# Writing the first batch of a fused attention and MoE kernel as one fixed order on five queues

## The chip, the core and the metric

The kernel runs on one core of a Trainium2 chip. The core has a matrix engine (TensorE, in the profile PE, with its weight loads as PEld) and three engines for other arithmetic: VectorE (DVE), ScalarE (ACT) and GpSimd (POOL). A fifth queue, SP, issues the transfers (DMA) between the chip's main memory and the core's memory. Each queue works strictly in its own order: an instruction that waits holds up everything behind it on the same queue. Only waits on other queues' results join them. The metric is the time of one execution in microseconds (us) on the device, taken from several runs.

## The reference

The inputs are `q`, `k`, `v` (8 batches, 8 heads, 576 rows, 64 columns), `p` (8, 8, 32, 64), and two weight matrices `w_in` (512 x 2048) and `w_out` (2048 x 512), which come as 64-bit floats.

```python
def sm_attn(qq, kk, vv):
    s = scale * np.matmul(qq, kk.transpose(0, 1, 3, 2))
    s = s - np.max(s, axis=-1, keepdims=True)
    a = np.exp(s)
    a = a / (np.sum(a, axis=-1, keepdims=True) + 1e-09)
    return np.matmul(a, vv)
p_packed = sm_attn(p, k, v)
out = sm_attn(q, p_packed, p_packed)
...
h = x @ w_in
relu6 = np.clip(h + 3.0, 0.0, 6.0)
g = h * relu6 / 6.0
return (g @ w_out)
```

`x` is the attention's result, its heads side by side: 4608 rows (8 batches of 576) of 512 columns.

## The kernel before

The 2048 columns between the two weight matrices are cut into 16 slices of 128; slice f is called **tile f** here. For each batch the kernel first does the attention. It never forms the attention's final product: the second softmax `a` (kept as `a_hi`, `a_lo`) is multiplied with `m`, the product of the packed values `pp` with `w_in`. Numbers are split into a rounded part and a rest (`hi`, `lo`), so each product is three matmuls.

**The first batch** is special, because the weights arrive while it runs. `first_attention` computes the attention of batch 0. `first_moe` then goes through the 16 tiles. Names for the steps of tile f, with their lines in the kernel before:

- **gemm1(f)** (L451, PE): 12 matmuls of 288 columns into the accumulator `ps_h`, of which there is one (`bufs=1`).
- **m0(f)** (`u_m0`, L196 PE, L207 ACT, L209 DVE): `m` for tile f. Its matmuls take one of two small accumulators (`ps_a0`, two buffers), which the attention of batch 1 uses as well.
- **relu(f)** (L954, ACT) and **stt(f)** (L955, DVE): the gate, read from `ps_h`. gemm1(f+1) can't start before stt(f) has let `ps_h` go.
- **gh(f)** (L963, ACT), the small `bnd_hi` (L964), and **gl(f)** (L965, POOL): the split of the gate.
- **gemm2(f)** (L856, PE): 12 matmuls of 512 columns. It stands one tile later in the order.
- **Narrowing in f** and **out f** (`narrowed`, L128): the 64-bit words of a slice of `w_in` or `w_out` become 32-bit: two passes on ACT (L142, L144), a shift on DVE (L148, after the first of the two passes), an add on POOL (L152). For `w_out` follow **wo_hi** (L162, ACT) and **wo_lo** (L164, on DVE, or on POOL for tiles 8 to 12).

The raw words land in two buffers each for `w_in` and `w_out` (`wp`, `bufs=2`); tiles 2 and 3 have places of their own. So the load of a slice waits on SP until the POOL add of the slice two before it is done.

**Attention of batch 1** runs between these tiles: transposes `tr` of the blocks of k and q on DVE (L401), scores **s1** (L268 PE, copies L284 ACT, maxima L285 DVE, exponentials L293 ACT), their transposes **et** (L307 PE, L308 ACT), the packed values **pv** (L323 PE), and the second scores **s2** (`u_s2`, L354): L268 on PE, then on DVE a transpose (L359); then, for each of two halves of the heads (`u_a`), a maximum and a subtraction (L367, L368, DVE), an exponential (L369, ACT), sum, add, reciprocal, product and transpose (L372 to L378, DVE), a_hi (L381, ACT) and a_lo (L383, DVE).

**What sets the order.** `first_attention` and the first four tiles stand in an order written out by hand on PE, DVE, ACT and POOL (`tc.manual_schedule(engines=HAND)`). From tile 4 on (`IN_ORDER = 4`) a scheduler, which has a model of its own of the times, orders these queues, and SP everywhere. `attend` hands it one and then two steps of the attention of batch 1 per tile. Batches 1 to 7 (`moe`, L864) are ordered by the scheduler before and after; there the attention of the next batch runs between tiles, as `fill` hands it out.

Of the kernel before, what the change touches and what calls it, by code (L numbers as in the profile page):

```python
# [36 lines left out]
def packed_attention_moe(  # L37
# [120 lines left out]
    def w_out_step(f):  # L158
# [5 lines left out]
        (nc.gpsimd if f in POOL else nc.vector).tensor_sub(out=wo_lo[:, f], in0=x, in1=wo_hi[:, f].bitcast(F32))  # L164
# [227 lines left out]

    def attention(b):


        def load(which, a):
            state["nat", which, b, a] = load_blocks(k if which == "k" else q, b, a)

        def turn(which, a):
            t = ap.tile([P, T, 32], F32, name="tr", tag="tr", bufs=4)  # L400
            nc.vector.transpose(out=t, in_=state.pop(("nat", which, b, a)))  # L401
            state[which, b, a] = t
# [56 lines left out]
    def first_attention():  # L459
# [336 lines left out]
        rest(m1)
        rest(b1)
        rest(wout0)
        step(wout1, 2)
        gemm1(h, 0, 1)  # L800
        warm(WARM[4])
        return h, {2: win2}, {1: wout1, 2: wout2}

    HAND = {mybir.EngineType.PE, mybir.EngineType.DVE, mybir.EngineType.Activation, mybir.EngineType.Pool}
# [92 lines left out]
    def first_moe(h, w_in, w_out):  # L897

        ahead = attention(1) if B > 1 else iter(())
        accs, m0 = [], {}  # L900
# [140 lines left out]
```

## Time and profile before

| what | value |
|---|---|
| median of 3 runs | 763.76 us (761.15 to 763.96) |
| the profiled execution | 758.97 us |
| its span, first to last instruction | 757.1 us |
| mean granted clock of TensorE | 0.995 of full |
| busy: PE, DVE, ACT, POOL | 739.4, 336.3, 387.6, 282.3 us |
| first product of batch 1 on PE starts | 138.26 us |

A row of the timeline has the start and the length in us, the queue, the line, the operation with its output and inputs, and in brackets how long the queue was idle before it and what ended the wait. Rows of equal instructions that follow each other are merged (x12). Float32 matmuls are counted twice each. A row of a window has its start and end, its length, the busy time of PE, PEld, DVE, ACT and POOL with counts, the granted clock of TensorE, the share of the DMA engines and GB/s. A row of a group has line, queue, operation, shapes and count, then busy us, mean ns of one, and the idle time before them. Lengths of instructions that follow each other overlap a little; the distance from start to start is what one costs.

### The profile page before, as it was taken

Reading aid. Unit: us, or ns where it says so; the run is one execution under the profiler, and the core shown is the slowest. Engines: PE = TensorE matmul, PEld = TensorE weight load, DVE = VectorE, ACT = ScalarE, POOL = GpSimd, SP = SyncE. Lnnn points to the kernel's source line nnn. Section 1 sums busy time; section 2 is a strip of 40 time slices with the busy share of each in tenths; the row PEclk is TensorE's granted clock in tenths of the full one; section 3 lists DMA queues with packets and bytes.
Section 4 is the critical chain, followed back from the end, with each engine's and each line's share of the span. In section 5 each row is a group of like instructions: output and inputs, shape, how many; then the busy total and the mean of one; then the engine's idle time right before and its main releaser. Section 6 shows DMA issues by size and latency. Waiting matters only on the chain.

```text
span 757.1 us, 13994 instructions
## 1 busy us (share of the span) xinstructions
PE 739.4 (98%) x5197; PEld 583.4 (77%) x5197; DVE 336.3 (44%) x709; ACT 387.6 (51%) x922; POOL 282.3 (37%) x420
## 2 busy tenths in 40 slices
PE   8998898999999999999999999999999999999998
PEld 6775675768777877888777886788787887888886
DVE  3676648432463355342733446342643527321121
ACT  4677864644455446463455535463354635553343
POOL 0487973423233233332333223333333333343332
PEclk9999899999999999999999999999999999999999
DMA  9859983104420532043310524024220210000010
GB/s 257 261 144 218 237 223 63 56 9 88 102 37 29 103 67 52 1 88 71 63 43 1 114 53 82 1 58 98 47 61 1 61 33 29 1 29 0 2 42 29
DMA packets 191205, 55.98 MB, mean 74 GB/s; under 512 B 173216, under 2 KB 184480, under 8 KB 191136
## 3 DMA queue, kind: packets, MB, share of 16 engines
q1 hardware_dynamic: 191136, 55.08, 31.6%
q8 instruction: 41, 0.67, 0.4%
q14 instruction: 28, 0.23, 0.1%
HBM read 45.61 MB, written 9.44 MB: 73 GB/s over the span
## 4 chain that ended last, share of the span: by engine, by line
PE 83%; DMA 5%; DVE 4%; SPq 3%; ACT 3%; issue 1%; POOL 1%; DVEq 0%; POOLq 0%; ACTq 0%
PE acc L856 47%; PE ps_hh L827 23%; PE ps L268 6%; SPq L216 2%; DMA raw_in<-in_moe_w_in_dram 2%; PE ps L323 2%; DMA nat<-in_k_dram 1%; PE ps_h L451 1%; DVE tr L401 1%; PE ps L307 1%; SPq L254 1%; POOL x_out L152 1%; PE ps_w L639 1%; DMA raw_out<-in_moe_w_out_dram 1%; DMA spare<-in_k_dram 1%
## 5 line engine op out<-in xcount | busy, mean ns | idle before, releaser
L845 POOL TENSOR_TENSOR g<-t,g 128x256 fp32r<-128x256 f32 x224 | 167.5, 751 | 410.7 <-ACT g L844 384.5
L856 PE MATMUL acc<-wo_hi,g 128*128 128x512 f32 x896 | 316.4, 394 | 1.3 <-ACT g L844 1.3
L840 DVE SCALAR_TENSOR_TENSOR t<-t,ps_hh 128x320 f32<-128x320 f32 (+1 forms) x224 | 100.1, 449 | 251.8 <-ACT t L839 251.6
L839 ACT ACTIVATE t<-ps_hh,three 128x320 f32<-128x320 f32 (+1 forms) x224 | 112.4, 503 | 177.9 <-PE ps_hh L827 169.8
L856 PEld LDWEIGHTS acc<-wo_hi,g 128*128 128x128 f32 x896 | 167.7, 188 | 35.4 <-issue 3.5
L856 PE MATMUL acc<-wo_lo,g 128*128 128x512 f32 x448 | 177.6, 396 | 0.0
L844 ACT CAST g<-t 128x256 fp32r<-128x256 f32 x224 | 90.4, 405 | 93.9 <-DVE t L840 92.6
L827 PE MATMUL ps_hh<-a_hi,m_hi 128*128 128x320 f32 (+1 forms) x448 | 136.2, 304 | 0.3 <-DVE t L840 0.3
L827 PE MATMUL ps_hh<-a_lo,m_hi 128*128 128x320 f32 (+1 forms) x448 | 132.7, 296 | 0.0
L827 PE MATMUL ps_hh<-a_hi,m_lo 128*128 128x320 f32 (+1 forms) x448 | 132.7, 296 | 0.0
L827 PEld LDWEIGHTS ps_hh<-a_hi,m_hi 128*128 128x128 f32 x448 | 84.4, 188 | 34.4 <-issue 19.9
L856 PEld LDWEIGHTS acc<-wo_lo,g 128*128 128x128 f32 x448 | 84.5, 189 | 12.4 <-issue 2.1
L827 PEld LDWEIGHTS ps_hh<-a_lo,m_hi 128*128 128x128 f32 x448 | 84.5, 189 | 8.2 <-issue 0.9
L827 PEld LDWEIGHTS ps_hh<-a_hi,m_lo 128*128 128x128 f32 x448 | 84.5, 189 | 1.6 <-issue 1.3
L401 DVE STREAM_TRANSPOSE tr<-nat 128x576 f32<-128x576 f32 x56 | 41.8, 765 | 30.2 <-DMA nat<-in_q_dram 12.8
L391 DVE TENSOR_TENSOR m_lo<-ps,m_hi 128x512 fp32r<-128x512 f32 x56 | 36.1, 684 | 35.1 <-ACT m_hi L390 35.1
L851 POOL TENSOR_TENSOR bnd_lo<-t,bnd_hi 128x64 fp32r<-128x64 f32 x112 | 39.1, 349 | 0.0
L390 ACT CAST m_hi<-ps 128x512 fp32r<-128x512 f32 x56 | 30.0, 589 | 9.9 <-PE ps_hh L827 8.1
L268 PE MATMUL ps<-w_in_sb,pps 64*32 64x512 f32 x448 | 34.3, 601 | 0.6 <-DVE m_lo L391 0.6
L856 PE MATMUL acc<-wo_hi,gh 128*128 128x512 f32 x64 | 26.7, 417 | 2.7 <-ACT gh L963 2.7
L152 POOL TENSOR_TENSOR w_in_sb<-w_in_sb,raw_in 128x512 int32<-128x512 int32 x14 | 18.9, 1347 | 27.7 <-ACT raw_in L144 19.2
L965 POOL TENSOR_TENSOR gl<-t,gh 128x512 fp32r<-128x512 f32 x16 | 22.0, 1373 | 17.6 <-ACT bnd_hi L964 11.0
...
## 6 DMA issues: line engine op xcount, KB each, us to landing
...
nat<-in_k_dram SPq DMA_DIRECT2D x112, 72.0 KB, 2.6
nat<-in_q_dram SPq DMA_DIRECT2D x112, 72.0 KB, 2.5
...
```

Source lines behind the costliest of these rows:

```text
L152: nc.gpsimd.tensor_tensor(out=xi, in0=xi, in1=low, op=ALU.add)
L268: nc.tensor.matmul(banks[x][NPK * a:NPK * a + NPK, :n], rows[half, a], c, start=True, stop=True)
L390: nc.scalar.copy(out=hi[:, x], in_=ps)
L391: nc.vector.tensor_sub(out=lo[:, x], in0=ps, in1=hi[:, x].bitcast(F32))
L401: nc.vector.transpose(out=t, in_=state.pop(("nat", which, b, a)))
L827: nc.tensor.matmul(h[:, :n], mm[:, g, fs], aa[:, t0:t0 + n], start=(g == 0 and i == 0), stop=(g == NG - 1 and i == 2),)
L839: nc.scalar.activation(out=t[:, :n], in_=h, func=AF.Relu, bias=three)
L840: nc.vector.scalar_tensor_tensor(out=t[:, :n], in0=t[:, :n], scalar=6.0, in1=h, op0=ALU.min, op1=ALU.mult)
L844: nc.scalar.copy(out=gh, in_=tm)
L845: nc.gpsimd.tensor_sub(out=gl, in0=tm, in1=gh.bitcast(F32))
L851: nc.gpsimd.tensor_sub(out=bnd_lo[:, slot:slot + REM], in0=tb, in1=bh.bitcast(F32))
L856: nc.tensor.matmul(acc, gg, ww[:, f], start=(f == 0 and i == 0), stop=(f == NF - 1 and i == 2),)
```

## The change

All of the first batch, `first_attention` and the 16 tiles, now stands in one written order, and on SP too. The diff, cut to what matters:

```diff
-WARM = (3, 2, 2, 1, 3)
+WARM = (3, 2, 2, 2)
...
-                raw = wp.tile([P, DM * (2 if wide_in else 1)], I32 if wide_in else F32, name=f"raw_{name}")
+                raw = wp.tile(
...
+                    bufs=3 if name == "in" else 2,
+                )
...
-        (nc.gpsimd if f in POOL else nc.vector).tensor_sub(out=wo_lo[:, f], in0=x, in1=wo_hi[:, f].bitcast(F32))
+        nc.vector.tensor_sub(out=wo_lo[:, f], in0=x, in1=wo_hi[:, f].bitcast(F32))
...
+    def first_parts(b):
...
+        return [
+            [[], [lambda: transpose_p(b), tn("k", 0), ld("k", 2), tn("k", 1), ld("k", 3)], []],
...
+            [[], [], [go(s2)]],
+            [[go(s2)], [], [go(s2)]],
+            [[go(s2)], [], [go(s2)]],
...
-        step(wout0, 3)
-        step(win1, 2)
...
+        load_w(4, ("in",))
+        if B > 1:
+            load_p(1)
+            load("k", 1, 0)
+            load("k", 1, 1)
...
-        win2, wout2 = w_in_step(2), w_out_step(2)
-        step(win2, 2)
-        step(wout2, 2)
...
-        def attend(f, n):
-            if f >= FIRST_AHEAD:
-                for _ in range(n):
-                    next(ahead, None)
+        def attend(f, place):
+            for part in plan[f][place] if f < len(plan) else ():
+                part()
...
-            if f == IN_ORDER:
-                hand.close()
...
-            step(in_(f + 2), 4)
...
-            rest(out_(f + 1))
-            step(out_(f + 2), 3 if f else 1)
...
+            attend(f, 1)
+            for i in (3, 4) if f == 3 else (f + (f > 3),):
+                rest(out_(i))
+            rest(in_(f + 2))
+            if f > 1:
+                more("in", f + 5)
+            for i in (3, 4) if f == 2 else (f + 1 + (f > 2),):
+                step(out_(i), 4)
+                if i not in (2, 3):
+                    more("out", 5 if i == 1 else i + 2)
             if last:
                 gemm2(*last)
...
+            with tc.issue_after(state["load"].ins):
+                for _ in range(PER_STEP if s < NF + FPC - 1 else 1000):
```

In tile f each queue now gets, in this order: the plan's first place; gemm1(f) and the matmuls of m0(f+1); relu, stt, the rest of m0(f+1), gh, bnd, gl; the plan's second place; wo_hi and wo_lo of tile f+1 (of tile f in tiles 0 to 2, of both 3 and 4 in tile 3); the narrowing of in f+2; the narrowing of out f+2 up to the POOL add (out f+1 in tiles 0 and 1, out 3 and out 4 in tile 2); gemm2(f-1); the plan's third place. The load of in f+5 is issued behind the narrowing of in f+2 (three buffers), that of out f+4 behind the narrowing of out f+2. The work of batch 2 is ordered behind the last weight load by `issue_after`; the scheduler still places it, on the five queues, between the written instructions. `warm` are matmuls on zeros.

The names in the rows below: `t` is the gate, `raw_140` and `raw_143` the raw words of tiles 2 and 3, `raw_in` and `raw_out` those of the others, `x_out` a narrowed slice of `w_out`, `z` and `at` the two forms of the second softmax. Lines of the changed kernel have other numbers: relu is L954 before and L987 after, stt L955 and L988, wo_hi L162 and L158, narrowing L142, L144, L148, L152 and L138, L140, L144, L148.

**ACT between relu(0) and relu(1).** Before:

```order
L954 ACTIVATE t<-ps_h_456,three 128x576
L162 CAST wo_hi<-x_out 128x512
L963 CAST gh<-t 128x512
L964 CAST bnd_hi<-t 128x64
L142 ACTIVATE raw_143<-raw_143 128x512
L144 ACTIVATE raw_143<-raw_143 128x512
L954 ACTIVATE t<-ps_h_534,three 128x576
```

After:

```order
L987 ACTIVATE t<-ps_h_456,three 128x576
L994 CAST gh<-t 128x512
L995 CAST bnd_hi<-t 128x64
L158 CAST wo_hi<-x_out 128x512
L138 ACTIVATE raw_140<-raw_140 128x512
L140 ACTIVATE raw_140<-raw_140 128x512
L138 ACTIVATE raw_out<-raw_out 128x512
L140 ACTIVATE raw_out<-raw_out 128x512
L987 ACTIVATE t<-ps_h_554,three 128x576
```

The narrowing of in 2 (`raw_140`) stood ahead of relu(0) before; it now stands behind gh(0) and wo_hi(0).

**ACT between relu(11) and relu(12).** Before:

```order
L954 ACTIVATE t<-ps_h_1314,three 128x576
L963 CAST gh<-t 128x512
L964 CAST bnd_hi<-t 128x64
L162 CAST wo_hi<-x_out 128x512
L142 ACTIVATE raw_in<-raw_in 128x512
L144 ACTIVATE raw_in<-raw_in 128x512
L142 ACTIVATE raw_out<-raw_out 128x512
L144 ACTIVATE raw_out<-raw_out 128x512
L207 CAST m_hi<-ps_1327 128x2x128
L162 CAST wo_hi<-x_out 128x512
L954 ACTIVATE t<-ps_h_1390,three 128x576
```

After:

```order
L987 ACTIVATE t<-ps_h_1324,three 128x576
L203 CAST m_hi<-ps_1337 128x2x128
L994 CAST gh<-t 128x512
L995 CAST bnd_hi<-t 128x64
L158 CAST wo_hi<-x_out 128x512
L138 ACTIVATE raw_in<-raw_in 128x512
L140 ACTIVATE raw_in<-raw_in 128x512
L138 ACTIVATE raw_out<-raw_out 128x512
L140 ACTIVATE raw_out<-raw_out 128x512
L377 CAST a_hi<-at 128x576
L987 ACTIVATE t<-ps_h_1388,three 128x576
```

A step of the second softmax of batch 1, a_hi, now stands between the narrowing and the next relu. Before, the exponentials and a_hi came after all narrowing of weights had ended.

**DVE around stt(12).** Before:

```order
L401 STREAM_TRANSPOSE tr<-nat 128x576 x2
L359 STREAM_TRANSPOSE z<-ps_1367 128x288
L359 STREAM_TRANSPOSE z<-ps_1366 128x288
L955 SCALAR_TENSOR_TENSOR t<-t,ps_h_1390 128x576
L367 TENSOR_REDUCE mx_1381<-z 128x18
L367 TENSOR_REDUCE mx_1448<-z 128x18
L209 TENSOR_TENSOR m_lo<-ps_1403,m_hi 128x2x128
L368 TENSOR_TENSOR z<-z,mx_1381 128x576
L401 STREAM_TRANSPOSE tr<-nat 128x576
```

After:

```order
L144 TENSOR_SCALAR x_out<-raw_out 128x512
L368 TENSOR_REDUCE den_1378<-z 128x18
L369 TENSOR_SCALAR den_1378<-den_1378 128x18
L370 RECIPROCAL den_1378<-den_1378 128x18
L371 TENSOR_TENSOR z<-z,den_1378 128x576
L374 STREAM_TRANSPOSE at<-z 128x576
L988 SCALAR_TENSOR_TENSOR t<-t,ps_h_1388 128x576
L205 TENSOR_TENSOR m_lo<-ps_1401,m_hi 128x2x128
L240 STREAM_TRANSPOSE p_tr<-p_nat 128x128
L160 TENSOR_TENSOR wo_lo<-x_out,wo_hi 128x512
L394 STREAM_TRANSPOSE tr<-nat 128x576
L144 TENSOR_SCALAR w_in_sb_1281<-raw_in 128x512
```

The first row after is the last shift of tile 11. The sum, product and transpose of the second softmax now stand behind it and ahead of stt(12); before, no shift of a weight was left here, and the second softmax was a step less far. The transposes `p_tr` and `tr` behind stt(12) belong to batch 2: after the change the shifts of tile 12 stand behind them, and on SP their loads stand behind the load of out 15, where before the loads of the first two blocks of k were issued among the weight loads.

More of the change, by code (lines that the diff above doesn't have):

```diff
@@ L391, in u_m, with load, turn @@
             nc.vector.tensor_sub(out=lo[:, x], in0=ps, in1=hi[:, x].bitcast(F32))
-    def attention(b):
[L396 to L402, printed above, removed]
+    def load(which, b, a):
+        state["nat", which, b, a] = load_blocks(k if which == "k" else q, b, a)
+    def turn(which, b, a):
+        t = ap.tile([P, T, 32], F32, name="tr", tag="tr", bufs=4)
+        nc.vector.transpose(out=t, in_=state.pop(("nat", which, b, a)))
+        state[which, b, a] = t
+    def attention(b):
         load_p(b)
-        load("k", 0)
-        load("k", 1)
+        load("k", b, 0)
+        load("k", b, 1)
         yield
         transpose_p(b)
-        turn("k", 0)
-        load("k", 2)
+        turn("k", b, 0)
+        load("k", b, 2)
         yield
-        turn("k", 1)
-        load("k", 3)
+        turn("k", b, 1)
+        load("k", b, 3)
         load_v(b, 0)
         yield
-        turn("k", 2)
-        load("q", 0)
+        turn("k", b, 2)
+        load("q", b, 0)
         yield
-        turn("k", 3)
-        load("q", 1)
+        turn("k", b, 3)
+        load("q", b, 1)
         yield
         yield from u_s1(b)
-        load("q", 2)
+        load("q", b, 2)
         yield
         yield from u_et(b, 0)
-        turn("q", 0)
+        turn("q", b, 0)
         yield
@@ L442, in attention, with ld, tn, go @@
         yield from u_s2(b)
+    def first_parts(b):
+        s1, s2, ppt = u_s1(b), u_s2(b), u_ppt(b)
+        et, pv = [u_et(b, x) for x in range(2)], [u_pv(b, x) for x in range(2)]
+        def ld(which, a):
+            return lambda: load(which, b, a)
+        def tn(which, a):
+            return lambda: turn(which, b, a)
+        def go(part, n=1):
+            return lambda: step(part, n)
+        def vs(x):
+            return lambda: load_v(b, x)
+        return [
+            [[], [lambda: transpose_p(b), tn("k", 0), ld("k", 2), tn("k", 1), ld("k", 3)], []],
+            [[], [vs(0)], [tn("k", 2), tn("k", 3)]],
+            [[ld("q", 0)], [ld("q", 1)], [go(s1)]],
+            [[], [], [go(s1)]],
+            [[go(s1)], [go(s1)], [go(s1), go(et[0], 2)]],
+            [[tn("q", 0)], [ld("q", 2)], [go(pv[0])]],
+            [[vs(1), go(pv[0])], [tn("q", 1), ld("q", 3)], [go(et[1], 2)]],
+            [[tn("q", 2)], [], [go(pv[1])]],
+            [[go(pv[1])], [tn("q", 3)], [go(ppt)]],
+            [[], [go(ppt)], [go(s2)]],
+            [[], [], [go(s2)]],
+            [[go(s2)], [], [go(s2)]],
+            [[go(s2)], [], [go(s2)]],
+            [[go(s2)], [], [go(s2)]],
+            [[go(s2)], [go(s2)], []],
+        ]
     def gemm1(h, f, g):
@@ L791, in first_attention @@
         gemm1(h, 0, 0)
+        step(m1)
+        step(wout0)
         step(b1, 4)
+        step(m1)
+        step(wout0, 2)
+        load_w(4, ("out",))
         warm(WARM[2])
         step(b1, 2)
+        rest(b1)
+        gemm1(h, 0, 1)
+        rest(m1)
         warm(WARM[3])
[L796 to L804, printed above, removed]
+        return h, {0: wout0}
+    HAND = {
+        mybir.EngineType.PE,
+        mybir.EngineType.DVE,
+        mybir.EngineType.Activation,
+        mybir.EngineType.Pool,
+        mybir.EngineType.SP,
+    }
     pend = []
@@ L895, in moe, with first_moe @@
                 second(2)
[L897 to L905 removed]
+    def first_moe(h, w_out):
+        plan = first_parts(1) if B > 1 else []
+        accs, w_in, m0 = [], {}, {}
+        def attend(f, place):
+            for part in plan[f][place] if f < len(plan) else ():
+                part()
         def gemm2(f, gh, gl):
@@ L970, in first_moe @@
             last = (f, gh, gl)
-            attend(f, PER_FIRST_STEP[1] if f < NF - 1 else 1000)
+            attend(f, 2)
         if B > 1:
@@ L1004, in fill @@
                 u_m(*soon.pop(0))
-            for _ in range(PER_STEP if s < NF + FPC - 1 else 1000):
-                if next(ahead, ahead) is ahead:
-                    break
+            with tc.issue_after(state["load"].ins):
+                for _ in range(PER_STEP if s < NF + FPC - 1 else 1000):
+                    if next(ahead, ahead) is ahead:
+                        break
         for c in range(2):
```

59 lines of the change are left out of this document (25 added, 34 removed).

## The prediction

> **What bounds the kernel now.** I read the page's busy times first, then windows of the span, then the timeline of PE in the first batch, then what ACT waited for. A row of a window is start:end, length, busy PE, PEld, DVE, ACT and POOL, granted clock, DMA share, GB/s.
>
> ```profile
> 36.90:138.40 101.50, 93.54 (x644) 69.38 (x645) 68.52 (x117) 71.55 (x144) 70.73 (x64) 0.97 0.73 166
> 138.40:757.10 618.70, 612.78 (x4255) 488.70 (x4253) 247.66 (x537) 295.81 (x734) 202.58 (x338) 1.00 0.22 48
> 36.90:42.13 5.23, 5.23 (x33) 4.33 (x33) 4.03 (x5) 3.67 (x8) 5.23 (x5) 1.00 0.82 156
> 75.00:78.00 3.00, 3.00 (x12) 1.92 (x12) 2.41 (x7) 1.79 (x5) 3.00 (x3) 0.61 1.02 374
> 86.40:90.00 3.60, 3.60 (x22) 3.11 (x19) 2.10 (x4) 2.97 (x7) 3.60 (x5) 0.60 1.14 349
> ```
>
> From 138.40 on PE is busy 612.78 of 618.70: PE sets that part, and the change leaves its matmuls as they are. The 16 tiles of the first batch run from 36.90 to 138.40. An undisturbed tile (third row: gemm1, m0 and gemm2 with nothing between) takes PE **5.23**; fifteen such tiles are 78, so 23 of the 101.5 go to the attention of batch 1 and to waits. Only there can the change act. Two waits were followed by a slow clock:
>
> ```profile
> 74.70 0.49 PE L856 MATMUL acc<-wo_hi,gh 128*128 128x512 f32 x1 [2.29 <-ACT gh L963]
> 85.40 1.07 PE L323 MATMUL ps<-v_nat,et 128*32 128x64 f32 x40 [2.03 <-ACT et L308]
> L142 ACT ACTIVATE raw_out<-raw_out 128x512 f32<-128x512 f32 x12 | 8.2, 685 | 4.2 <-DMA raw_out<-in_moe_w_out_dram 4.0
> L142 ACT ACTIVATE raw_in<-raw_in 128x512 f32<-128x512 f32 x12 | 8.1, 678 | 6.9 <-DMA raw_in<-in_moe_w_in_dram 6.8
> ```
>
> PE waited 2.29 and 2.03, and the clock then stood at 0.61 for 3.0 and 0.60 for 3.6: a further 3.0·0.39 = 1.2 and 3.6·0.40 = 1.4. ACT waited 6.8 and 4.0 for raw weights. These are what the third buffer, the earlier weight loads and the later loads of batch 2 can take away.
>
> **The loop of a tile.** In the written order relu(f) to relu(f+1) is a chain on ACT, with stt on DVE inside it:
>
> ```profile
> 35.31 0.74 ACT L954 ACTIVATE t<-ps_h,three 128x576 f32<-128x576 f32 x1 [1.55 <-PE ps_h L451]
> ...
> 47.02 0.62 ACT L162 CAST wo_hi<-x_out 128x512 fp32r<-128x512 f32 x1 [0.99 <-POOL x_out L152]
> 47.54 0.68 ACT L142 ACTIVATE raw_out<-raw_out 128x512 f32<-128x512 f32 x1
> 48.68 0.61 ACT L963 CAST gh<-t 128x512 fp32r<-128x512 f32 x1
> 49.34 0.69 ACT L142 ACTIVATE raw_in<-raw_in 128x512 f32<-128x512 f32 x1
> 50.48 0.72 ACT L954 ACTIVATE t<-ps_h,three 128x576 f32<-128x576 f32 x1
> ...
> 36.09 0.76 DVE L955 SCALAR_TENSOR_TENSOR t<-t,ps_h 128x576 f32<-128x576 f32 x1 [0.53 <-ACT t L954]
> ```
>
> Starts give the cost: gh and bnd 49.34-48.68 = 0.66, wo_hi 0.52, each narrowing 1.14. gh now stands right behind stt, so it starts 0.78 + 0.76 + 0.02 = 1.56 after relu. A tile's ACT loop is 1.56 + 0.66 + 0.52 + 2·1.14 = **5.02**, just under PE's 5.23; before, narrowing filled the wait for stt. Whatever the plan puts on ACT or DVE into this loop makes it longer than PE's.
>
> **Part 1, tiles 0 and 1.** in 2 is now narrowed behind gh(0) and wo_hi(0).
>
> ```profile
> 36.67 1.30 POOL L152 TENSOR_TENSOR w_in_sb<-w_in_sb,raw 128x512 int32<-128x512 int32 x1
> 37.38 1.14 DVE L164 TENSOR_TENSOR wo_lo<-x_out,wo_hi 128x512 fp32r<-128x512 f32 x1 [0.54 <-ACT wo_hi L162]
> 36.90 0.40 PE L451 MATMUL ps_h<-a_hi,m_hi 128*128 128x288 f32 x1 [0.33 <-DVE t L955]
> 38.67 0.66 PE L196 MATMUL ps<-w_in_sb,pp_bd 128*64 128x128 f32 x8
> ```
>
> gemm1(1) stays at 36.90: it waits for stt(0), so the two warming matmuls that go were no part of the path. relu(0) stays at 35.31. gh(0) then starts at 36.9, wo_hi(0) at 37.5, in 2 is through its two passes at 39.3. DVE meanwhile does, from 36.85, the transposes of p, k0 and k1 (0.76 each for k by its group in part 4, taken together at 1.7), then wo_lo(0) at 1.14 to 39.7, the shift at 0.43 to 40.1; POOL adds in 1.30 to 41.4. PE wants m0(2) at 38.67: it waits **2.7**, where it waited for nothing. Bounds: 2.0 if wo_lo takes less beside POOL, 3.5 if k1 lands late. A gap of that size cost clock above, 1.3 on average: **+4.0** in all; gemm2(0) stands behind m0(2) and pays too. relu(2) comes at 47.9.
>
> [...]
>
> **Part 2, tiles 2 to 4.** The attention's instructions join the loop.
>
> ```profile
> L284 ACT COPY e<-ps 128x288 f32<-128x288 f32 x4 | 1.4, 392 | 0.0
> L293 ACT ACTIVATE e<-e,nb 128x576 f32<-128x576 f32 x2 | 1.5, 768 | 0.0
> L308 ACT COPY et<-ps 128x512 f32<-128x512 f32 x2 | 1.2, 582 | 0.3 <-PE ps L307 0.3
> 54.69 1.54 DVE L148 TENSOR_SCALAR x_out<-raw_out 128x512 int32<-128x512 int32 x1
> 57.28 0.43 DVE L148 TENSOR_SCALAR x_out<-raw_out 128x512 int32<-128x512 int32 x1 [0.72 <-ACT raw_out L142]
> ```
>
> Tile 2: 5.02, a second out (1.14), two copies of e (0.7) = 6.85. Tile 3: 5.02, a second wo_hi (0.5), copies 0.7, the last maximum and bias on DVE 0.65, an exponential 0.75, and 0.7 for a shift that meets POOL's add (0.43 alone, 1.54 in the worst row) = 8.35. Tile 4: 5.02, the second exponential behind its bias 1.25, the copy of et 0.5 = 6.8. So relu(5) at 47.9 + 22.0 = **69.9**. PE can't run ahead: m0(4), m0(5) and m0(6) need a small accumulator that s1 or et holds until ACT's copies.
>
> **Part 3, tiles 5 to 9.** Here PE's path is the longer. From relu(5): copy of et done 0.1, then 5.23 and pv 1.07 to the end of gemm1(6); four more tiles of 5.23, with pv 1.07 and, taken from it, et 0.8 and a half of s2 0.7 (5 and 8 matmuls against pv's 20): relu(10) at 69.9 + 6.4 + 23.6 = **99.9**.
>
> **Part 4, tiles 10 to 13.** The second softmax stands behind the last shift of a tile on DVE, and its ACT step ahead of the next relu.
>
> ```profile
> L359 DVE STREAM_TRANSPOSE z<-ps 128x288 f32<-128x288 f32 x4 | 1.6, 447 | 0.0
> L367 DVE TENSOR_REDUCE mx<-z 128x18 f32<-128x576 f32 x2 | 1.4, 739 | 0.0
> 124.74 0.73 DVE L368 TENSOR_TENSOR z<-z,mx 128x576 f32<-128x576 f32 x1
> L369 ACT ACTIVATE z<-z 128x576 f32<-128x576 f32 x2 | 1.4, 680 | 1.7 <-DVE z L368 1.7
> L372 DVE TENSOR_REDUCE den<-z 128x18 f32<-128x576 f32 x2 | 1.5, 726 | 0.0
> L374 DVE RECIPROCAL den<-den 128x18 f32<-128x18 f32 x2 | 0.4, 232 | 0.0
> L375 DVE TENSOR_TENSOR z<-z,den 128x576 f32<-128x576 f32 x2 | 1.4, 748 | 0.0
> L378 DVE STREAM_TRANSPOSE at<-z 128x576 f32<-128x576 f32 x2 | 1.5, 766 | 0.0
> L381 ACT CAST a_hi<-at 128x576 fp32r<-128x576 f32 x2 | 1.4, 678 | 1.7 <-DVE at L378 1.7
> L383 DVE TENSOR_TENSOR a_lo<-at,a_hi 128x576 fp32r<-128x576 f32 x2 | 1.6, 790 | 0.0
> L401 DVE STREAM_TRANSPOSE tr<-nat 128x576 f32<-128x576 f32 x12 | 8.9, 758 | 2.3 <-DMA nat<-in_q_dram 1.6 <-DMA nat<-in_k_dram 0.6
> ```
>
> relu to the end of the last shift is 1.56 + 0.66 + 0.52 + 1.14 + 0.68 + 0.43 = 5.0. From there to the next relu: tile 10, two transposes 0.85, maximum 0.7, subtraction 0.7, exponential 0.6: **7.85**. Tile 11, 0.7 + 0.2 + 0.2 + 0.75 + 0.75 and a_hi 0.6 = 3.2: **8.2**. Tile 12, a_lo, maximum, subtraction, exponential 2.8 and two transposes of batch 2 1.5: **9.3**. Tile 13, as 11 and one transpose: **8.9**. Sum 34.2, where PE needs 4·5.23 + 0.7 = 21.6. The last shift always follows POOL's add of the same tile's in: 0 to 1.1 each, I take 0.7, **+2.8**.
>
> ```profile
> 107.39 0.92 SPq L236 DMA_DIRECT2D p_nat<-in_p_dram  x2
> 119.10 4.09 SPq L216 DMA_DIRECT2D nat<-in_k_dram  x8
> nat<-in_k_dram SPq DMA_DIRECT2D x112, 72.0 KB, 2.6
> ```
>
> Batch 2's p and k are issued behind out 15, whose buffer comes free 7.0 after relu(11): then 0.4, p 1.85, four blocks of k 2.05, landing 2.6 = 13.9 after relu(11), 5.0 after relu(12). DVE reaches that transpose 3.5 after relu(12): a wait of 0 to 3, I take **1.5**. relu(14) at 99.9 + 34.2 + 2.8 + 1.5 = **138.4**.
>
> **The end.** stt(14) and m_lo 1.9, gemm1(15) and gemm2(14) 4.6, two blocks of m for batch 1 of 1.0 each, gemm2(15) 2.9 (its 512 columns' share of 4.6): 149.8.
>
> ```profile
> 140.11 1.09 PE L268 MATMUL ps<-w_in_sb,pps 64*32 64x512 f32 x16
> ```
>
> Batch 1 began at 138.3 before with one of these blocks still to do (1.1): 139.4. The change is **10.4 later**, at a span of 767.5 and 769.4 for the profiled execution of 758.97. That execution lies 4.8 under the median of the runs; on the median: 763.76 + 10.4 = **774**. Weight loads have 3 tiles (in) or 2 (out) of lead, above 10 us, against landings of about 6; wo_lo of tiles 8 to 12 on DVE (0.7 to 1.1) is in the loops of part 4 beside ACT's passes. Both at nothing; if a load came late by 1.5 in six tiles, +9.
>
> **Rivals.**
> 1. *Faster*: the loops of tiles 10 to 13 hide behind PE. If each stays under PE's 5.9, PE's path alone counts: 36.9 + 14·5.23 + 6.5 for the attention's matmuls (two pv, two et, four halves of s1 and s2) + 4.0 from part 1 + 4.6 + 2.1 + 2.9 at the end = 130.2, 9.2 earlier: 755. For it: ACT's waits for weights (10.8) and the clock's 2.6 go. Against: in-order queues, 3 us of DVE behind the last shift.
> 2. *No change*: parts 1 and 2 cost half (relu(10) at 95) and nothing meets on DVE and POOL: 95 + 34.2 + 11.4 = 140.6, 1.2 later, 765. For it: shifts of 0.43 do occur.
> 3. *Much slower*: k of batch 2 lands 3 later at each of its first two transposes, and the clock drops in the gaps before the end: +6, 780. For it: PE would idle 3 to 4 in each of four tiles.
> 4. *It doesn't do what it says*: the third buffer is free of effect because out keeps two and sets the pace; it alone would leave 764 and belongs to case 2.
>
> **How the numbers follow.** The forecast 0.57, rival 3 0.11, rival 2 (and 4) 0.17, rival 1 0.15. A difference under 0.5% (3.8 us) can't be told from none here. Faster by more: rival 1 and 0.01 of 2, 0.16. Within: 0.15, nearly all of rival 2. Slower: the rest of 2 (0.01), the forecast and rival 3, 0.69. The sum's own bounds are -7.6 (clock 1.3, half of part 2's surplus over PE 2.0, port 2.8, k 1.5) and +5.2 (port 1.6, k 1.5, m0(2) 0.8, a slow clock at the end 1.3): 766 to 779 for the forecast alone. With rival 2 and the near end of rival 1, and half of rival 3, the range is 758 to 781.
>
> **What would show it.** PE waits about 2.7 for m0(2) on POOL, then a low clock; relu(11) to relu(14) start 8 to 10 apart, each behind `z` or `a_hi` on ACT; DVE waits for k in tile 12; batch 1's first product near 149. Wrong if relus stay under 6 apart in tiles 10 to 13.

## The result and the profile after

| | before | changed |
|---|---|---|
| median, runs of one session | 762.45 us (4 runs) | 769.89 us (4 runs, 768.09 to 771.25) |
| ratio | | 1.0125, 95% interval 1.0095 to 1.0155 |
| the profiled execution | 758.97 us | 771.25 us |
| its span | 757.1 us | 769.4 us |
| mean granted clock | 0.995 | 0.986 |
| busy: PE, DVE, ACT, POOL | 739.4, 336.3, 387.6, 282.3 us | 739.0, 342.7, 387.5, 279.1 us |

The change is slower, by 7.4 us between the medians and 12.3 between the two profiled spans, of which the changed kernel's is the longest of its four, while the profiled execution of before is shorter than any of its four runs. The forecast was 10.4 later and 774. The places came out almost as worked out, but two sizes were wrong in opposite directions, so part of the agreement is luck.

Windows of the changed kernel, in the columns of the windows shown before: the first batch, the rest, and the five stretches with a low clock.

```profile
36.90:153.90 117.00, 97.74 (x671) 75.54 (x672) 76.55 (x128) 77.30 (x155) 70.31 (x61) 0.91 0.61 151
153.90:769.40 615.50, 608.82 (x4227) 486.16 (x4225) 246.66 (x535) 293.86 (x730) 201.30 (x336) 1.00 0.22 48
41.00:48.00 7.00, 6.16 (x20) 4.78 (x21) 4.48 (x7) 4.01 (x9) 5.59 (x6) 0.52 0.93 189
72.00:75.50 3.50, 3.50 (x10) 2.75 (x9) 2.48 (x5) 2.81 (x7) 2.47 (x3) 0.52 0.77 214
119.50:123.50 4.00, 4.00 (x11) 3.17 (x12) 2.58 (x4) 1.57 (x3) 0.46 (x1) 0.57 0.49 151
130.00:133.50 3.50, 3.14 (x13) 2.43 (x14) 3.19 (x5) 0.56 (x1) 2.07 (x2) 0.52 0.73 129
140.00:144.00 4.00, 4.00 (x17) 3.06 (x14) 2.55 (x4) 1.57 (x3) 0.94 (x1) 0.57 0.36 58
```

Nearly all of the loss lies ahead of 153.9, where batch 1's first product starts with gemm2(15) done. Before, that product started at 138.26, but one block of `m` (140.11) and all of gemm2(15) still stood behind it:

```profile
141.13 0.50 PE L856 MATMUL acc<-wo_hi,gh 128*128 128x512 f32 x1
143.98 0.30 PE L827 MATMUL ps_hh<-a_hi,m_hi 128*128 128x320 f32 x1
```

The point of before that has the same work behind it is therefore 138.26 + 1.1 + 2.85 = 142.2, and the first batch has become 11.7 longer; another 0.6 came after it.

PE's waits in the timeline (in brackets: how long, and on whom), and the starts of the relus from tile 9 on:

```profile
41.84 1.12 PE L192 MATMUL ps<-w_in_sb,pp_bd 128*64 128x128 f32 x8 [2.96 <-POOL w_in_sb L148]
71.06 0.66 PE L192 MATMUL ps<-w_in_sb,pp_bd 128*64 128x128 f32 x8 [1.79 <-ACT et L304]
118.76 0.66 PE L192 MATMUL ps<-w_in_sb,pp_bd 128*64 128x128 f32 x8 [2.68 <-POOL w_in_sb L148]
130.36 1.12 PE L192 MATMUL ps<-w_in_sb,pp_bd 128*64 128x128 f32 x8 [4.79 <-POOL w_in_sb L148]
139.75 0.72 PE L192 MATMUL ps<-w_in_sb,pp_bd 128*64 128x128 f32 x8 [2.72 <-POOL w_in_sb L148]
...
96.79 0.74 ACT L987 ACTIVATE t<-ps_h,three 128x576 f32<-128x576 f32 x1
103.87 0.74 ACT L987 ACTIVATE t<-ps_h,three 128x576 f32<-128x576 f32 x1 [1.59 <-PE ps_h L482]
112.58 0.72 ACT L987 ACTIVATE t<-ps_h,three 128x576 f32<-128x576 f32 x1
122.01 0.73 ACT L987 ACTIVATE t<-ps_h,three 128x576 f32<-128x576 f32 x1
133.54 0.72 ACT L987 ACTIVATE t<-ps_h,three 128x576 f32<-128x576 f32 x1
142.98 0.74 ACT L987 ACTIVATE t<-ps_h,three 128x576 f32<-128x576 f32 x1
```

Before, PE's longest waits in the tiles were 2.29, 2.03 and 1.75. Now m0(13), m0(14) and m0(15) wait 2.68, 4.79 and 2.72 for POOL's add, which is the end of a chain that starts at a late relu: relu(11) to relu(14) are 9.43, 11.53 and 9.44 apart.

What makes the relus late stands on DVE. From the timelines of DVE and POOL, tiles 10 to 12:

```profile
110.34 1.62 DVE L364 TENSOR_TENSOR z<-z,mx 128x576 f32<-128x576 f32 x1
119.08 1.50 DVE L371 TENSOR_TENSOR z<-z,den 128x576 f32<-128x576 f32 x1
124.94 0.31 DVE L240 STREAM_TRANSPOSE p_tr<-p_nat 128x128 f32<-128x128 f32 x1 [1.07 <-DMA p_nat<-in_p_dram]
127.75 0.78 DVE L394 STREAM_TRANSPOSE tr<-nat 128x576 f32<-128x576 f32 x1 [1.57 <-DMA nat<-in_k_dram]
129.09 1.83 DVE L379 TENSOR_TENSOR a_lo<-at,a_hi 128x576 fp32r<-128x576 f32 x1
...
110.04 1.29 POOL L148 TENSOR_TENSOR x_out<-x_out,raw_out 128x512 int32<-128x512 int32 x1
118.67 1.29 POOL L148 TENSOR_TENSOR x_out<-x_out,raw_out 128x512 int32<-128x512 int32 x1
128.97 1.34 POOL L148 TENSOR_TENSOR w_in_sb<-w_in_sb,raw_in 128x512 int32<-128x512 int32 x1 [2.61 <-issue]
130.27 1.80 POOL L148 TENSOR_TENSOR x_out<-x_out,raw_out 128x512 int32<-128x512 int32 x1
```

The subtraction that took 0.73 before takes 1.62 where POOL's add of out is running, the product there 1.50, and a_lo beside the add of in 1.83; and two transposes of batch 2 wait for their loads. ACT had waited 10.8 for raw weights. The groups of its first narrowing pass in the tiles now show no wait:

```profile
L138 ACT ACTIVATE raw_out<-raw_out 128x512 f32<-128x512 f32 x13 | 8.7, 667 | 0.0
L138 ACT ACTIVATE raw_in<-raw_in 128x512 f32<-128x512 f32 x12 | 8.1, 674 | 0.0
```

The loads come in time, but the time was not set by them any more.

### The profile page after: what moved, and what is told of

It reads as the page before. It is cut to its first block, busy times and chain, and to the rows that moved or that the text cites. A ratio compares the mean times of both kernels' runs of the same rounds, so it can differ in the third digit from the quotient of the medians.

```text
span 769.4 us, 13995 instructions
## 1 busy us (share of the span) xinstructions
PE 739.0 (96%) x5193; PEld 586.4 (76%) x5193; DVE 342.7 (45%) x714; ACT 387.5 (50%) x922; POOL 279.1 (36%) x415
## 3 DMA queue, kind: packets, MB, share of 16 engines
HBM read 45.61 MB, written 9.44 MB: 72 GB/s over the span
## 4 chain that ended last, share of the span: by engine, by line
PE 83%; ACT 5%; DVE 4%; DMA 3%; SPq 2%; issue 2%; POOL 1%; DVEq 0%; ACTq 0%; POOLq 0%
PE acc L893 48%; PE ps_hh L864 23%; PE ps L264 6%; PE ps L319 2%; DMA nat<-in_k_dram 1%; SPq L212 1%; PE ps_h L482 1%; DMA raw_in<-in_moe_w_in_dram 1%; PE ps L303 1%; DVE t L988 1%; ACT t L987 1%; DVE tr L394 1%; POOL w_in_sb L148 1%; ACT wo_hi L158 1%; DMA spare<-in_k_dram 1%
## 5 line engine op out<-in xcount | busy, mean ns | idle before, releaser
L264 PE MATMUL ps<-w_in_sb,pps 64*32 64x512 f32 x448 | 32.7, 601 | 0.0
L893 PE MATMUL acc<-wo_hi,gh 128*128 128x512 f32 x64 | 30.1, 470 | 0.0
L148 POOL TENSOR_TENSOR w_in_sb<-w_in_sb,raw_in 128x512 int32<-128x512 int32 x14 | 19.3, 1377 | 25.6 <-ACT raw_in L140 17.8
```

The source lines that it names most:

```text
L148: nc.gpsimd.tensor_tensor(out=xi, in0=xi, in1=low, op=ALU.add)
L264: nc.tensor.matmul(banks[x][NPK * a:NPK * a + NPK, :n], rows[half, a], c, start=True, stop=True)
L893: nc.tensor.matmul(acc, gg, ww[:, f], start=(f == 0 and i == 0), stop=(f == NF - 1 and i == 2),)
```

## The experiments

All ratios are to the kernel before, timed on the same chip in the same session. The table has the distances between the starts of successive relus in one profiled execution of each kernel; "5-9" is a sum of five, "all" is relu(0) to relu(15), "rest" is from relu(15) to the end of the span. In eight profiles with an unchanged first attention relu(0) itself lies anywhere from 34.50 to 36.70, so spans are not compared closer than that.

| kernel | ratio | tile 1 | 2 | 3 | 4 | 5-9 | 10 | 11 | 12 | 13 | 14 | all | rest |
|---|---|---|---|---|---|---|---|---|---|---|---|---|---|
| before | 1 | 5.97 | 5.43 | 7.23 | 6.57 | 39.30 | 5.15 | 9.77 | 6.83 | 4.85 | 5.57 | 100.4 | 621.4 |
| changed | 1.0125 | 9.55 | 6.71 | 7.83 | 6.29 | 33.05 | 8.71 | 9.43 | 11.53 | 9.44 | 3.61 | 111.2 | 622.8 |
| 1 | 1.0068 | 5.32 | 9.86 | 7.84 | 6.30 | 31.52 | 8.71 | 9.41 | 11.51 | 9.46 | 3.60 | 107.4 | 622.5 |
| 2 | 1.0105 | 6.50 | 7.96 | 7.80 | 6.31 | 33.09 | 8.70 | 9.41 | 9.16 | 9.42 | 3.63 | 107.0 | 628.2 |
| 3 | 1.0002 | 6.49 | 7.52 | 7.81 | 6.30 | 31.47 | 5.98 | 5.61 | 5.93 | 8.04 | 9.25 | 99.4 | 622.6 |
| 4 | 0.9920 | 5.55 | 9.37 | 7.83 | 6.29 | 31.55 | 5.98 | 5.61 | 5.94 | 5.90 | 5.93 | 93.8 | 625.3 |
| 5 | 1.0077 | 5.01 | 7.33 | 7.80 | 6.29 | 31.48 | 8.71 | 9.41 | 11.51 | 9.45 | 3.61 | 104.5 | 622.4 |
| 6 | 1.0080 | 8.04 | 6.69 | 7.85 | 6.30 | 31.51 | 8.67 | 9.40 | 9.16 | 9.39 | 3.61 | 105.6 | 623.5 |
| 7 | 1.0250 | 9.31 | 6.71 | 7.80 | 7.79 | 40.62 | 8.67 | 9.42 | 12.21 | 11.29 | 3.61 | 122.4 | 621.4 |
| 8 | 0.9897 | 5.10 | 7.32 | 7.82 | 6.29 | 31.48 | 5.97 | 5.58 | 5.97 | 5.92 | 5.92 | 91.3 | 622.4 |
| 9 | 1.0005 | 6.04 | 5.38 | 6.92 | 5.37 | 42.91 | 6.00 | 5.82 | 8.31 | 5.54 | 5.27 | 101.3 | 620.9 |
| 10 | 1.0121 | 9.37 | 6.72 | 7.80 | 6.31 | 33.72 | 9.25 | 9.99 | 10.09 | 9.85 | 3.61 | 111.7 | 622.1 |
| 11 | 1.0080 | 7.95 | 6.73 | 7.78 | 6.32 | 33.07 | 8.67 | 9.40 | 11.54 | 9.55 | 3.66 | 109.7 | 621.5 |
| 12 | 1.0075 | 6.47 | 6.97 | 7.80 | 6.29 | 31.52 | 8.70 | 9.39 | 11.48 | 9.44 | 3.62 | 106.7 | 622.6 |

The first two rows show that the change also won something: from relu(5) to relu(10) it takes 6.2 less than before, against 6.4 more from relu(0) to relu(5) and 10.5 more from relu(10) to relu(15).

### 1. In 2 narrowed early again

```diff
         step(wout0)
+        win2 = w_in_step(2)
+        step(win2, 2)
         warm(WARM[1])
...
         rest(b1)
+        rest(win2)
         gemm1(h, 0, 1)
...
```

> The changed kernel with one step put back: the two ACT passes of in 2 are issued in the first attention again, its shift and its add ahead of tile 0. Theory L (the end of the first batch is set by the chain relu to relu, and a delay early in it is handed down to the end): in the changed kernel m0(2) waits 2.96 and the clock is then 0.50 for 6.3 us, in which m0(2) and gemm2(0) take 6.3 where 3.4 is normal. Without the wait relu(2) comes at about 44.5 instead of 49.99, and the whole program ends 5 to 5.9 earlier: about 764.5, ratio to the kernel before about 1.005. Rival S (the delay is swallowed later, since the weight loads, the k and q blocks or PE's own path set tiles 5 to 9): relu(2) comes early all the same, but relu(10) stays near 103 and the end moves by at most 1: ratio 1.011 to 1.0125.

Measured: 766.45 (before 760.16), ratio 1.0068 (1.0044 to 1.0092). The wait for m0(2) is gone and relu(2) comes 9.2 after relu(0), not 14.6. But relu(3) takes 9.86, and the end gains less than tile 1 did. DVE in this kernel:

```profile
44.08 0.78 DVE L394 STREAM_TRANSPOSE tr<-nat 128x576 f32<-128x576 f32 x1 [0.95 <-DMA nat<-in_k_dram]
46.44 0.78 DVE L394 STREAM_TRANSPOSE tr<-nat 128x576 f32<-128x576 f32 x1 [1.58 <-DMA nat<-in_k_dram]
47.14 0.72 DVE L991 SCALAR_TENSOR_TENSOR t<-t,ps_h 128x576 f32<-128x576 f32 x1
```

The transposes of batch 1's blocks k2 and k3 stand ahead of stt(2), and wait for their loads; stt(2) starts 4.0 after relu(2), not 0.8. So half of theory L and half of rival S hold: the first wait counts, and a late load takes part of it back.

### 5. The same, and k2, k3 behind m_lo

```diff
-            [[], [vs(0)], [tn("k", 2), tn("k", 3)]],
-            [[ld("q", 0)], [ld("q", 1)], [go(s1)]],
+            [[], [vs(0)], []],
+            [[], [tn("k", 2), tn("k", 3), ld("q", 0), ld("q", 1)], [go(s1)]],
```

> In 2 early as in the first experiment, and besides, the transposes of batch 1's blocks k2 and k3 taken from the end of tile 1, ahead of the product of tile 2 on DVE, and put into tile 2 behind m_lo (with the loads of q0 and q1 behind them). In the first experiment relu(2) came 9.2 after relu(0), 5.3 sooner than in the changed kernel, but relu(3) only 9.9 after that, since DVE stood 0.95 and 1.58 for these blocks with the product of tile 2 queued behind. Theory K (the gain was swallowed by this wait for a load): relu(2) to relu(3) falls to about 7, relu(14) comes about 2.5 to 3 earlier than there; about 763.5, ratio about 1.004. Rival: something else in tile 2 holds it (its seven ACT passes and the scores' maxima), relu(2) to relu(3) stays above 9 and the ratio at 1.007.

Measured: 765.53 (before 759.76), ratio 1.0077 (1.0056 to 1.0098). In the profile tile 2 falls from 9.86 to 7.33 and relu(0) to relu(15) by 2.9 against the first experiment, as theory K has it. In the times it doesn't show, and the ratio is the rival's 1.007, not the theory's 1.004: the two intervals overlap, and 2.9 is 0.4%. The cause of the long tile 2 is shown by the profile, its worth in the median is not.

### 2 and 6. The transposes of batch 2, held back on DVE

```diff
-            nc.vector.scalar_tensor_tensor(out=tv, in0=tv, scalar=6.0, in1=hv, op0=ALU.min, op1=ALU.mult)
+            state["stt"] = nc.vector.scalar_tensor_tensor(out=tv, in0=tv, scalar=6.0, in1=hv, op0=ALU.min, op1=ALU.mult)
...
-            with tc.issue_after(state["load"].ins):
+            with tc.issue_after(state["load"].ins), tc.issue_after(state["stt"].ins):
```

In the sixth, `state["gate"]` stands in place of `state["stt"]`: the last `m_lo` of batch 1's first block.

> The changed kernel with one condition more: on DVE the work of batch 2 may not be placed ahead of the product of tile 15, so the transposes of its p and of four blocks of its k leave tiles 12 and 13; the loads stay where they are. Theory L: in the changed kernel they stand on DVE between relu(12) and relu(14) with 3.4 of their own time and 4.0 of waits for their loads, on the way to the next relu. relu(12) to relu(13) goes from 11.5 to about 8, relu(13) to relu(14) from 9.4 to about 8.4; the end is 4 to 5 earlier: about 765.5, ratio about 1.0065. Rival W (DVE would have waited there anyway, for ACT's wo_hi or for PE, so the transposes fill holes): under 1 earlier, ratio 1.011 to 1.0125. If batch 2 then starves later, the gain comes back as PE waits after 160.

> The changed kernel with batch 2's work held on DVE behind the first block of m of batch 1 (its m_lo), not just behind the product of tile 15 as in the second experiment. There relu(12) to relu(13) fell from 11.5 to 9.2, but the transposes, now between the last product and m_lo, made PE wait 3.1 in batch 1 and the clock was low for 7. Theory G (what batch 2's transposes cost in tiles 12 and 13 is 2 to 3, and it is won if they stand where nobody waits): relu(15) as in the second experiment, and less than 1 of new waits in batch 1: 2 to 4 faster than the changed kernel, ratio 1.007 to 1.010. Rival: batch 1's own first products need DVE at that place as much, PE waits 2 or more for them: ratio 1.0105 or more, as before.

Measured: 769.53 (before 760.16), ratio 1.0105 (1.0065 to 1.0146), and 766.23 (before 759.76), ratio 1.0080 (1.0059 to 1.0101). Both take 2.4 from tile 12 (11.53 to 9.16) and nothing from tile 13, where DVE had time to spare. In the second experiment they come back after relu(15), as a wait of PE and a slow clock behind it:

```profile
155.77 0.64 PE L864 MATMUL ps_hh<-a_hi,m_hi 128*128 128x320 f32 x1 [3.08 <-DVE t L877]
...
155.00:162.00 7.00, 6.23 (x19) 5.65 (x20) 2.66 (x5) 4.05 (x13) 3.00 (x6) 0.51 0.40 106
```

Its rest is 628.2, against 623.5 in the sixth, where nothing that PE waits for is queued behind the transposes. So batch 2's transposes cost 2.4 in these tiles by the profiles. That it can be had in the time as well is likely (1.0080 against 1.0125), but the intervals overlap.

### 3. The second softmax in smaller pieces

`u_a` is cut at each DVE piece and each ACT pass, and `first_parts` places the pieces (`a0`, `a1`: the two halves):

```diff
-            [[], [], [go(s2)]],
-            [[go(s2)], [], [go(s2)]],
-            [[go(s2)], [], [go(s2)]],
-            [[go(s2)], [], [go(s2)]],
-            [[go(s2)], [go(s2)], []],
+            [[], [], [go(s2, 2), go(a0)]],
+            [[], [go(a0)], [go(a0), go(a1)]],
+            [[], [go(a1)], [go(a1), go(a0)]],
+            [[], [go(a0)], [go(a0), go(a1)]],
+            [[], [go(a0), go(a1)], [go(a0), go(a1)]],
+            [[], [go(a1, 2)], []],
```

> The changed kernel with the second softmax of batch 1 in smaller pieces: in each of tiles 10 to 15 one DVE piece behind m_lo and ahead of wo_lo, one or two behind the last shift, and its ACT passes at the end of a tile's narrowing or behind bnd, never between a DVE piece of the same tile and the next relu; same instructions, same sizes. Theory L (the relu of the next tile waits for a chain DVE, ACT, that was put ahead of it): tiles 10 to 13 take 6 to 8 each instead of 8.7, 9.4, 11.5 and 9.4, the sum goes from 39.1 to about 30, the program ends about 9 earlier: near 761, ratio about 1.0. Rival P (it is the amount of work on DVE beside POOL's that counts, not its place: DVE pieces take up to twice their time beside POOL): the pieces get longer where they now stand, the sum stays above 36, ratio above 1.008.

Measured: 762.29 (before 760.16), ratio 1.0002 (0.9977 to 1.0027): the whole loss is gone with the place of these instructions alone. Tiles 10 to 13 take 25.6 together, not 39.1, and after tile 9 m0 waits long only once, m0(15) for 3.21. The two subtractions, now behind m_lo:

```profile
106.95 0.75 DVE L390 TENSOR_TENSOR z<-z,mx 128x576 f32<-128x576 f32 x1
112.88 0.75 DVE L390 TENSOR_TENSOR z<-z,mx 128x576 f32<-128x576 f32 x1
113.73 1.62 DVE L160 TENSOR_TENSOR wo_lo<-x_out,wo_hi 128x512 fp32r<-128x512 f32 x1
```

The subtractions take 0.75 there, ahead of POOL's gl, and wo_lo behind the second pays some of it (1.62). In the eighth kernel, which has the pieces in the same places, both products take 0.75 (at 118.24 and 125.09). PE's m0(13) and m0(14) now wait 0.74 and 0.67 for the adds of in, where they waited 2.68 and 4.79. Rival P falls: a piece can still get longer, but the sum is 25.6, not above 36. Batch 2's transposes are now met in tiles 13 and 14 (8.04 and 9.25).

### 4 and 8. All together

The fourth kernel is the first three edits in one, the eighth the first, third, fifth and sixth.

> The three edits together (in 2 early, batch 2's transposes behind tile 15 on DVE, the second softmax in smaller pieces). Theory L: relu(2) at 44.5, tiles 10 to 13 at 5.5 to 6.5 each (sum near 24), so relu(14) at 143.0 - 5.5 - 15 = about 122.5 and the end about 20 under the changed kernel: near 750, ratio 0.982 to 0.988 to the kernel before. Rivals S and P: the parts don't add, PE's own path and DVE's sum set the tiles: relu(14) stays above 130, ratio 0.995 or more.

> In 2 early, k2 and k3 behind m_lo of tile 2, the second softmax in smaller pieces, and batch 2 on DVE behind the first block of m of batch 1. By the parts: the fourth experiment was 755.5 (0.992), tile 2 took 9.4 there and should take 7, and its PE waits of 2.0 after tile 15 with a low clock of 3.4 after them should go: 3 to 5 earlier, about 751.5, ratio 0.986 to 0.989. Rival: tile 2 keeps its length, or the later k of batch 2 makes PE wait further on: no better than 0.992.

Measured: 755.51 (before 760.16), ratio 0.9920 (0.9889 to 0.9952), and 752.06 (before 759.76), ratio 0.9897 (0.9875 to 0.9918). Both are faster than the kernel before and the changed one, and both fall short of what I expected (0.982 to 0.988, and 0.986 to 0.989). In the fourth, tile 2 still takes 9.37, and its rest is 625.3. Tiles 10 to 14 of the eighth take 5.6 to 6.0 each. The window of the 15 tiles and the group of m0's matmuls of this kernel:

```profile
36.72:128.00 91.28, 82.20 (x621) 64.98 (x620) 65.94 (x115) 72.17 (x145) 68.31 (x59) 1.00 0.71 181
L192 PE MATMUL ps<-w_in_sb,pp_bd 128*64 128x128 f32 x112 | 9.2, 285 | 8.3 <-POOL w_in_sb L148 5.9 <-ACT et L304 1.8 <-DVE mx L281 0.6
```

No low clock is left, and m0's waits are 8.3. In the changed kernel the same group had 18.6:

```profile
L192 PE MATMUL ps<-w_in_sb,pp_bd 128*64 128x128 f32 x112 | 10.2, 307 | 18.6 <-POOL w_in_sb L148 15.5 <-ACT et L304 1.8 <-DVE mx L281 1.3
```

### 7 and 9. The third buffer

```diff
-                    bufs=3 if name == "in" else 2,
+                    bufs=2,
```

and, in the ninth, the kernel before with `bufs=3 if name == "in" else 2` and nothing else.

> The changed kernel with two buffers for raw w_in in place of three, nothing else. The prediction's fourth rival and its sum say that the third buffer changes nothing by itself: a load of in has a lead of two tiles, above 10, against a landing of 3.8. Then the time is that of the changed kernel within 1.5: ratio 1.0105 to 1.0145. Rival Q: with two buffers the load of in f+5 waits at the head of SP's queue for one tile, and batch 1's v and q and the weights of out behind it come late: ACT waits for raw_out or raw_in, tiles 3 to 7 get longer by 3 or more, ratio 1.017 or more.

> One part alone: the kernel before, with three buffers for raw w_in and nothing else (its order is still found by the scheduler, which then starts loads of in earlier and moves narrowing, transposes and weight loads against each other). ACT waits 6.8 there for raw_in, so a gain of 0 to 6 is on offer. Theory L: in the changed kernel the buffer was worth 9.8 because the loads stand in SP's queue in a written order and a load without a buffer held up v and the weights of out behind it; where loads are placed when their buffers are free, it is worth little: ratio 0.992 to 1.003. Rival: the buffer is a gain of its own, and the order took it back: ratio under 0.99.

Measured: 779.25 (before 759.76), ratio 1.0250 (1.0225 to 1.0275); and 761.23 (before 759.90), ratio 1.0005 (0.9979 to 1.0032). In the written order the third buffer is worth 1.25%, 9.5 us, where I had put nothing; in the scheduler's order no worth shows beyond the noise. The POOL add that frees a buffer, SP's queue behind it, and PE in the seventh kernel:

```profile
86.14 1.43 POOL L148 TENSOR_TENSOR w_in_sb<-w_in_sb,raw_in 128x512 int32<-128x512 int32 x1 [0.42 <-ACT raw_out L138]
...
87.60 0.38 SPq L121 DMA_DIRECT2D raw_in<-in_moe_w_in_dram  x1
88.02 0.50 SPq L121 DMA_DIRECT2D raw_out<-in_moe_w_out_dram  x1
88.63 4.33 SPq L250 DMA_DIRECT2D v_nat<-in_v_dram  x5
...
93.83 0.32 PE L319 MATMUL ps<-v_nat,et 128*32 128x64 f32 x8 [2.60 <-DMA v_nat<-in_v_dram]
```

The add ends at 87.57. The load of in waits at the head of the queue until then; out's weights and v, which have their places free, go out behind it. In the changed kernel the same five loads of v went out at 79.18. PE waits 3.4 for v in four pieces, ACT 5.9 for raw_out. Rival Q holds.

### 10. wo_lo of tiles 8 to 12 on POOL again

```diff
-        nc.vector.tensor_sub(out=wo_lo[:, f], in0=x, in1=wo_hi[:, f].bitcast(F32))
+        (nc.gpsimd if 8 <= f < 13 else nc.vector).tensor_sub(out=wo_lo[:, f], in0=x, in1=wo_hi[:, f].bitcast(F32))
```

> The changed kernel with wo_lo of tiles 8 to 12 on POOL, as before the change. The prediction costed this move at nothing. On DVE a wo_lo takes 1.28 beside POOL and ends 0.1 to 0.2 after ACT's pass over raw_in, so on DVE nothing waits for it; on POOL it stands between bnd_lo and the add of in, for which PE waits in tiles 10 to 13. Theory N: relu(9) to relu(14) takes as long as before within 1, or up to 1.3 a tile longer where PE waits for the add of in: ratio 1.011 to 1.018. Rival D (DVE's work is what sets tiles 10 to 13): each of them 0.6 to 1.3 shorter, the sum from 39.1 to about 35, ratio about 1.008.

Measured: 769.83 (before 759.90), ratio 1.0121 (1.0093 to 1.0150). Tiles 10 to 13 take 39.2 against 39.1: 0.4 to 0.6 more in three of them, 1.4 less in tile 12. The term of nothing was right.

### 11 and 12. PE kept busy in the wait for m0(2)

```diff
             for g in range(NG):
                 gemm1(h, f, g)
+            if f == 1:
...
+                for _ in range(WG):
+                    nc.tensor.matmul(accs[3][:, :2 * P], zeros[:, :P], zeros, start=True, stop=True)
             step(m_(f + 1))
```

> The changed kernel with ten matmuls of 256 columns on zeros into an accumulator of the second product that is not in use yet, between the first product of tile 1 and m0(2): they fill 2.6 of the 2.8 to 3.0 in which PE waits for the add of in 2, and delay nothing. In three other kernels with the same order up to there, relu(1) to relu(2) took 6.5, 6.5 and 8.0, and in the changed kernel's profile 9.55, with a low clock of 0, 0, 3.5 and 7.0. Theory C (the wait costs a low clock in some executions and in others not): with PE kept busy relu(1) to relu(2) is 6.5, m0(2) and gemm2(0) at full clock; over the runs 1 to 2 faster: ratio 1.010 to 1.011, spread of the runs smaller. Rival: the low clock there isn't due to the wait, relu(1) to relu(2) is 8 to 9.5 again.

> The eleventh experiment again with six such matmuls. A float32 matmul runs as two here, so ten took 4.48 and m0(2) came 1.45 late (relu(1) to relu(2) 7.95), though the clock stayed at 1.00. Six take 2.7, just the wait of 2.76. Theory C: clock 1.00 from 36 to 48, relu(1) to relu(2) 6.5, against 9.55, 6.5, 6.5, 8.0, 9.3 and 9.4 in the six profiles of kernels that have this order without the filling (a mean of 1.7 above 6.5): 1 to 2 faster than the changed kernel over the runs, ratio 1.0085 to 1.011. Rival: the clock falls all the same, relu(1) to relu(2) is 8 or more.

Measured: 767.13 (before 759.90), ratio 1.0080 (1.0055 to 1.0106), with ten; 766.53 (before 760.38), ratio 1.0075 (1.0047 to 1.0103), with six. The twelfth kernel in this place:

```profile
39.99 2.75 PE L985 MATMUL acc<-pps 128*128 128x256 f32 x12
42.94 0.66 PE L193 MATMUL ps<-w_in_sb,pp_bd 128*64 128x128 f32 x8 [0.20 <-POOL w_in_sb L149]
...
36.00:48.00 12.00, 10.98 (x65) 9.10 (x63) 8.12 (x13) 8.79 (x17) 7.68 (x7) 1.00 0.92 204
```

The clock is 1.00 throughout, in the eleventh too, and tile 1 takes 6.47 though m0(2) starts as late as it did. (With ten, tile 1 took 7.95: the filling itself came 1.45 too long.) The ratios lie further below the changed kernel's than the 1 to 2 us that I expected, but the intervals overlap, so the gain over the runs is likely and not shown. The mean granted clock of the runs points the same way: 0.986 to 0.990 in the changed kernel's four runs, 0.990 to 0.996 in the fifteen with the filling.

## Why the prediction was right, and where it was not

| step of the prediction | predicted | measured in the changed kernel |
|---|---|---|
| m0(2) waits for POOL's add | 2.7 | 2.96 |
| slow clock behind it | 1.3 | 3.05 here; 0, 0, 1.5, 2.8 and 2.9 in kernels 2, 3, 6, 7, 10 with this order up to there |
| tiles 2, 3, 4 | 6.85, 8.35, 6.8 | 6.71, 7.83, 6.29 |
| tiles 5 to 9 | 30.0 | 33.05; 31.5 without a slow clock (kernels 1, 3, 6, 12) |
| tile 10, 11 with 0.7 for POOL's add | 8.55, 8.9 | 8.71, 9.43 |
| tile 12, with that and 1.5 for k | 11.5 | 11.53 |
| tile 13, with that | 9.6 | 9.44 |
| relu(14) to the start of batch 1 | 11.4 | 10.95 |
| that start, and the like point of before | 149.8 and 139.4 | 153.9 and 142.2 |

**Part 1** held: the wait is where it was said and as long, and the first experiment takes it away. Its clock term was a mean over a lottery. Six profiles have the same instructions up to there and the same wait of 2.7 to 3.0; two show no low clock, the others one of 3.5 or 7.0. It also read the two drops as too cheap, since its windows of before stand beside them: from 75.5 to 79.0 the clock is 0.52 and from 85.5 to 89.5 it is 0.57, so each costs 1.7, not 1.2 and 1.4. Experiments 11 and 12 point to the wait as the cause: with it filled, neither profile has the drop, against four of six without. By relu(3) the loss is smaller, since tile 2 takes 6.71 in the changed kernel, where DVE does not wait for k at all, and 7.96 and 7.52 in kernels 2 and 3: tiles 1 and 2 together are 16.3 in the changed kernel, 14.5 and 14.0 in kernels 2 and 3.

**Part 2** was right to 0.5 a tile.

**Part 3** is the term that was too small by 3.05. 1.6 of it is a slow clock in tile 5, behind a wait of 1.79 for the copy of et (8.15, where it is 6.5 to 6.6 without it). The other 1.4 was left out: I let PE run alone there, but m0 waited for POOL's add twice in these tiles as well (0.64 at 85.21 and 1.05 at 97.74).

**Part 4** carries the loss, as said, and the sum of four tiles is 39.1 against 38.5. The third experiment shows it: with the same work in other places the ratio is 1.0002. Inside, one price stood in the wrong place. The last shift lost nothing to POOL's add of in: it starts ahead of it, not behind it as I had it (108.49 against 108.65 in tile 10), took 0.41 to 0.43 in all four tiles, and ends 5.0 after relu in tiles 10, 11 and 13, as worked out. It was the softmax's own subtraction, products and a_lo, behind the shift, that met POOL's adds: 0.9 more for the subtraction, 0.75 for each of two products, 1.0 for a_lo, 3.4 in all where I had 2.8. The wait for k was 1.57 in tile 12 (1.5 predicted), and experiments 2 and 6 give 2.4 for batch 2's transposes there.

In tile 10 POOL's add runs from 110.04 to 111.33, the subtraction starts at 110.34 and ends at 111.96, 0.63 after the add; with POOL idle it took 0.71 (132.20). The prediction's bounds call this term "port"; no run shows a port, only rows that are longer beside POOL's add, by the 3.4 above.

**The end** has the plain mistake. The step took "138.3 and one block of m, 1.1" for the like point of before; gemm2(15) was also still to come there, 2.85. With it the prediction's own terms give 149.8 - 142.2 = 7.6 later, and the profile shows 11.7. So the hit of 10.4 on 12.3 is a sum that was 4.1 short (relu(2) 2.1, tiles 2 to 4 -1.2, tiles 5 to 9 3.05, tiles 10 to 13 0.6, the end -0.45) and a mark that was 2.8 off the other way; the last 0.6 came behind it. On the medians, 7.4, the corrected sum would have been nearer. (Part 3's four tiles add up to 23.5 from their own terms, not 23.6; nothing hangs on it.)

**Weight loads** were put at nothing, and with three buffers ACT waited for none in the tiles. But the reason for the fourth rival, that the buffer is free of effect because out sets the pace, fell: with two buffers the changed kernel's ratio is 1.025.

**Rivals.** The first priced tiles that hide behind PE at 755, 9 faster, with part 1's 4.0 still in it. The change as it stood did not meet its condition, each loop under PE's 5.9. The eighth kernel nearly meets it, with 5.6 to 6.0, and is 7.7 faster (752.06 against 759.76), but it has part 1's wait taken out as well, so it is near that price and no proof of it. The second rival had relu(10) at 95; it came at 103.87. The third had k land 3 later twice; DVE's waits for k ahead of relu(13) were 1.57 and 0.31.

**Open.** The rest after relu(15) is 621 to 624 in all profiles but those of kernels 2 and 4, without a cause that I could name for the spread, and the start of relu(0) moves by 2.2 between kernels that are alike up to there.
